# Windowed attention with sinks, then a two-layer MLP, on one core: masks added on PE in batch 0, dummy PE passes, and double-buffered transposed q and k

## The chip, the core and the metric

The kernel runs on one core of a Trainium2 chip. The metric is device microseconds (us) per execution, the median of several runs. The engines are PE (TensorE), DVE (VectorE), ACT (ScalarE), POOL (GpSimd) and SP (SyncE, which here only issues DMAs).

## What is computed

Batch 4, 8 heads, 768 positions, head dimension 64. Each query sees the first 4 positions (the sinks) and the last 128 positions up to its own. The attention output, laid out as 3,072 tokens by 512, goes through an MLP with 2,048 hidden units and a squared ReLU.

```python
scores = q @ k.T / sqrt(64)
keep = is_sink | ((pos_q - pos_k >= 0) & (pos_q - pos_k < 128))
a = softmax(where(keep, scores, -1e9))
x = (a @ v).transpose(0, 2, 1, 3).reshape(3072, 512)
out = relu(x @ w_in) ** 2 @ w_out
```

## The kernel before

The work goes batch by batch (b = 0 to 3). `attention(b)` makes the 512-wide input of batch b's MLP, `layer1` and `layer2` are the MLP. Attention of batch b + 1 is laid between the MLP matmuls of batch b, so that PE has work while ACT and DVE do the softmax.

**Order.** The program is not written in the order in which it runs. Each step is registered with a key (its due time), the engines that may do it with a cost for each, the steps it comes after, and the buffers (`Slot`) that it takes and gives back. `Plan.run` (line 52) then walks a model of the engines, and records at each point the step that can start first. So costs and keys set the order of each engine's instructions; on the chip each engine runs its own instructions in that order, and waits on semaphores for the others.

**Inputs.** In batches 0 and 1, q and k are loaded in FP32 on SP's queue (`load_qk`, L303), cast to BF16 with the pairs of heads regrouped (`regroup`, tile `qs`, on ACT, DVE or POOL, L186, L188, L190), transposed on PE (`transpose`, tile `pt`, L405) and copied to `qkT_sb` (`unload`). Batch 0 does it in two groups: positions 0 to 511 first (its loads are the first DMAs), then positions 512 to 767, whose loads stand behind the first half of `w_in`. That half is issued on POOL's queue once v's second block of batch 0 has landed (`load_w_in`, L271). In batches 2 and 3 (`NATURAL`) the DMAs do this: POOL's queue loads q, k and v as BF16 (`load_natural`, L335, L342; q and k to tiles `qn`), and SP's queue transposes each 128 positions into `qkT_sb` (`turn`, L379), twelve transfers a batch. There is one `qkT_sb`; the turns of batch b wait until all scores and sink scores of batch b - 1 have been computed (`prev_scores`, `prev_sinks`).

**Attention.** For each 256 positions s and each pair m0 of head pairs: `scores` (tile `ps`, L484) on PE, into two PSUM slots of the pool `att`; `expo` (tile `expm`, L500) on ACT; `domask`, a multiplication with a 0/1 mask on DVE (L509), or two affine_selects on POOL (L202); `values` on PE (tile `po`, L535), with the sinks' part from `es`; `norm` on DVE (L547, L549): two reciprocals and two multiplications into `xn_sb`. The sink scores of a batch are four matmuls (`sink_scores`, tile `pk`, L454); they read all positions of the transposed q. `bridge` (tile `px`, L571) and its copy, or a DMA transpose in batches 2 and 3 (`turn_x`, L560), give `xT`.

**MLP.** `layer1` (tile `pm`, L594), ReLU (L603, L605), square (L610); `layer2` (tile `py`, L630), copy to `osb`, store (L647). PSUM has two pools, `att` and `den`, of two slots each.

```python
prev_scores = [ops[x] for x in ops if x[0] == "scores" and x[1] == b - 1]
...
ops["turn", b, ti, t] = op(
    at(0.1 * s), {"sp": 1.25}, turn, dma=0.3, reads=[qn_slot[b, ti, s]],
    after=[ops["qk", b, ti, t]] + prev_scores + prev_sinks)
...
load_w_in(0, 5.7, ("v", 0, 1))
load_w_in(1, 8.7)
```

Of the kernel before, what the change touches and what calls it, by code (L numbers as in the profile page):

```python
# [18 lines left out]
DMA_LATENCY = 2.0  # L19


class Slot:


    def __init__(self, pool, readers):
        self.pool, self.readers, self.end = pool, readers, 0.0
# [10 lines left out]
class Plan:  # L37
# [14 lines left out]
    def run(self):  # L52
# [71 lines left out]
def kernel(  # L124
# [11 lines left out]
    nc = tc.nc  # L136
# [16 lines left out]
    sizes = dict(att=2, den=2, qr=5, qs=6, vf=3, qn=8, expm=8, r=3, osb=2)  # L153
# [10 lines left out]
    mask0 = consts.tile([128, 2, 4, 128], BF16)  # L164
    head_rows = consts.tile([32, H, 1], BF16)
# [6 lines left out]
    qkT_sb = consts.tile([128, NP, 2, S], BF16)  # L172
# [27 lines left out]
    def triangles(e_tile, i, n):  # L200

        nc.gpsimd.affine_select(  # L202
            out=e_tile, in_=e_tile, compare_op=ALU.is_ge, fill=0.0, base=i - 1,
            pattern=[[0, n], [1 if i else -1, 128]], channel_multiplier=-1 if i else 1,
        )

    def fill(e):
        nc.vector.memset(ident, 1.0)
        nc.vector.memset(tri, 1.0)
# [11 lines left out]
    def build_triangles(e):  # L221
        for i in range(2):
            triangles(tri[:, i:i + 1, :], i, 1)

# [18 lines left out]
    c_tri = op(-0.9, {"pool": 0.6}, build_triangles)  # L243
    c_masks = op(-0.9, {"dve": 1.5}, build_masks, after=[c_tri])
    c_sinks = op(-0.8, {"pool": 0.5}, build_head_rows)
# [78 lines left out]
    def load_natural(b, s, older_values):  # L324

        begun = [ops["layer1", b - 2, 0, 0], w_out_op[3]]
        for ti in (1, 0):
            sl = qn_slot[b, ti, s] = Slot("qn", 2)
            for i in range(2):
                t = 2 * s + i  # L330

                def run(e, i=i, t=t, ti=ti):
                    if i == 0:
                        qn_t[b, ti, s] = work["qn"].tile([128, 2, DM], BF16, name="qn", tag="qn")
                    return [nc.gpsimd.dma_start(  # L335
                        out=qn_t[b, ti, s][:, i, :].rearrange("p (h d) -> p h d", d=D),
                        in_=(q, k)[ti][b, :, 128 * t:128 * t + 128, :].rearrange("h p d -> p h d"))]
                o = dma_op("pool", ("qk", b, ti, t), run, 64 * 0.032, takes=[sl] if i == 0 else ())
# [10 lines left out]
    def attention(b, key):  # L349
# [5 lines left out]
        prev_scores = [ops[x] for x in ops if x[0] == "scores" and x[1] == b - 1]  # L355
        prev_sinks = [ops[x] for x in ops if x[0] == "sinks" and x[1] == b - 1]
# [402 lines left out]
```

## Time and profile before

| what | value |
|---|---|
| median of 3 runs | 247.62 us (247.38 to 248.05) |
| the profiled execution | 247.71 us, of which the span of the trace is 246.0 us |
| PE busy | 217.8 us (89%) |
| ACT, DVE, POOL busy | 119.7 us (49%), 110.5 us (45%), 48.2 us (20%) |
| PE's idle time by stretch: 0 to 24, 24 to 54, 54 to 104, 104 to 117, 117 to 200, 200 to 246 us | 10.9, 3.5, 0.5, 7.0, 1.1, 5.2 us |
| mean granted TensorE clock | 0.979 |
| DMA | 29.68 MB, mean 121 GB/s |

PE is the engine with the most work, so the reading starts at the stretches in which it is idle or slow: at the start, where data arrive, and between 104 and 117 us. Some matmul records are missing in the last stretch, so its idle time is overstated. The granted clock is recorded from about 25 us on; ahead of that the durations of equal matmuls tell which of the two levels (1.2 and 2.4 GHz) was in force.

### The profile page before, as it was taken

What the parts mean: (1) busy time and instruction counts of PE and PEld (TensorE: products, weight loads), DVE (VectorE), ACT (ScalarE), POOL (GpSimd) and SP (SyncE); (2) the same over time, 40 slices, a digit from 0 to 9 for tenths busy, and PEclk for the clock granted to TensorE, in tenths of its full rate; (3) what the DMA queues carried; (4) which work ended last, traced back from release to release, by engine and by line L of the source; (5) the groups of instructions that cost most, each with busy time, mean ns of one, the idle gap of its engine ahead of it and who ended that gap; (6) DMA issues with size and microseconds to landing.
All of it is one profiled execution on the core that took longest, in us unless ns stands there. A gap on an engine that the chain in (4) does not pass through costs nothing.

```text
span 246.0 us, 4463 instructions
## 1 busy us (share of the span) xinstructions
PE 217.8 (89%) x1838; PEld 130.5 (53%) x1860; DVE 110.5 (45%) x251; ACT 119.7 (49%) x137; POOL 48.2 (20%) x67
## 2 busy tenths in 40 slices
PE   1469789979999999944999999999999999999983
PEld 1246668967454654422854554467555544584431
DVE  6476379776434527540343352573633413431010
ACT  3477367887335464740433534765731335560110
POOL 2021153492632933552000000000000100000000
PEclk9999979999999999995999999999999999999999
DMA  5979999899991999999801266644004222000051
GB/s 172 284 130 212 270 323 319 181 173 184 149 131 7 217 110 170 149 154 149 41 18 26 89 171 87 171 85 45 0 3 128 88 43 85 1 3 0 0 209 47
DMA packets 82500, 29.68 MB, mean 121 GB/s; under 512 B 70192, under 2 KB 78384, under 8 KB 82480
## 3 DMA queue, kind: packets, MB, share of 16 engines
q0 software_dynamic: 40608, 8.92, 51.3%
q1 hardware_dynamic: 41872, 20.49, 35.6%
q8 instruction: 14, 0.23, 0.4%
q14 instruction: 6, 0.05, 0.1%
HBM read 27.30 MB, written 6.29 MB: 137 GB/s over the span
## 4 chain that ended last, share of the span: by engine, by line
PE 77%; DMA 14%; ACT 3%; issue 2%; DVE 1%; SPq 1%; DVEq 0%; ACTq 0%
PE py L630 33%; PE pm L594 32%; PE po L535 5%; PE ps L484 4%; DMA w_in_sb<-in_moe_w_in_dram 4%; DMA qr<-in_k_dram 4%; DMA qkT_sb<-qn 4%; DMA vf<-in_v_dram 3%; ACT r L603 2%; PE pk L454 2%; PE pt L405 1%; ACT qs L186 1%; DVE qkT_sb L188 1%; SPq L379 1%; PE px L571 1%
## 5 line engine op out<-in xcount | busy, mean ns | idle before, releaser
L594 PE MATMUL pm<-xT,w_in_sb 128*128 128x256 bf16 (+1 forms) x570 | 89.7, 313 | 1.0 <-ACT r L603 0.7
L630 PE MATMUL py<-w_out_sb,gT_sb 128*128 128x512 bf16 x369 | 86.3, 379 | 1.9 <-DVE osb L188 0.8
L594 PEld LDWEIGHTS <-w_in_sb 128*128 128x128 bf16 x576 | 56.6, 100 | 30.3 <-issue 3.4
L603 ACT ACTIVATE r<-pm 128x1024 bf16<-128x1024 f32 x45 | 46.0, 1026 | 40.9 <-PE pm L594 35.1
L630 PEld LDWEIGHTS <-gT_sb 128*128 128x128 bf16 x384 | 35.6, 98 | 41.2 <-issue 3.0
L500 ACT ACTIVATE expm<-ps 128x1024 bf16<-128x1024 f32 (+1 forms) x48 | 43.1, 950 | 27.4 <-PE ps L484 27.4
L610 DVE TENSOR_TENSOR gT_sb<-r 128x1024 bf16<-128x1024 bf16 x48 | 33.7, 703 | 48.7 <-ACT r L603 48.6
L509 DVE TENSOR_TENSOR expm<-expm,mask 128x1024 bf16<-128x1024 bf16 (+1 forms) x44 | 28.1, 641 | 24.9 <-ACT expm L500 23.8
L202 POOL TENSOR_SCALAR_AFFINE_SELECT expm<-expm 128x512 bf16<-128x512 bf16 x8 | 5.3, 690 | 97.4 <-ACT expm L500 97.4
L186 ACT ACTIVATE osb<-py 128x1024 f32<-128x1024 f32 (+1 forms) x10 | 9.6, 959 | 23.8 <-PE py L630 16.3
L535 PEld LDWEIGHTS <-expm 128*128 128x128 bf16 x352 | 18.4, 101 | 4.6 <-DVE xn_sb L549 0.3
L484 PE MATMUL ps<-qkT_sb 64*128 64x128 bf16 (+1 forms) x256 | 16.0, 258 | 3.9 <-DVE qkT_sb L188 2.3
L535 PE MATMUL po<-v,expm 128*128 128x65 bf16 x352 | 19.3, 200 | 0.0
L549 DVE TENSOR_TENSOR xn_sb<-po,rc 128x256 bf16<-128x256 f32 x48 | 18.1, 418 | 0.0
L405 PE MATMUL pt<-ident,qs 128*128 128x128 bf16 x96 | 9.1, 250 | 8.7 <-ACT qs L186 5.2
L484 PEld LDWEIGHTS <-qkT_sb 64*128 64x128 bf16 x256 | 9.1, 99 | 13.0 <-issue 10.2
L188 DVE COPY osb<-py 128x1024 f32<-128x1024 f32 (+2 forms) x4 | 3.6, 892 | 26.0 <-PE py L630 26.0
L535 PE MATMUL po<-vs,es 128*128 128x65 bf16 x128 | 14.0, 195 | 0.0
L335 POOL DMA_DIRECT2D qn<-in_k_dram x12 | 10.6, 892 | 13.6 <-DMA qkT_sb<-qn 8.3
L547 DVE RECIPROCAL rc<-po 128x4 f32<-128x4 f32 x48 | 5.9, 165 | 15.3 <-PE po L535 15.3
L405 PEld LDWEIGHTS <-qs 128*128 128x128 bf16 x96 | 6.8, 111 | 10.5 <-ACT qs L186 5.5
L535 PEld LDWEIGHTS <-es 128*128 128x128 bf16 x128 | 12.3, 101 | 0.0
(40 smaller groups left out, 98.6 us busy)
## 6 DMA issues: line engine op xcount, KB each, us to landing
out_dram<-osb SPq DMA_DIRECT2D x11, 512.0 KB, 3.2
vf<-in_v_dram SPq DMA_DIRECT2D x12, 256.0 KB, 7.9
w_in_sb<-in_moe_w_in_dram POOLq DMA_DIRECT2D x2, 1024.0 KB, 11.1
w_out_sb<-in_moe_w_out_dram POOLq DMA_DIRECT2D x4, 512.0 KB, 8.9
qr<-in_k_dram SPq DMA_DIRECT2D x2, 768.0 KB, 9.0
qr<-in_q_dram SPq DMA_DIRECT2D x2, 768.0 KB, 10.6
qn<-in_k_dram POOLq DMA_DIRECT2D x12, 128.0 KB, 11.0
qn<-in_q_dram POOLq DMA_DIRECT2D x12, 128.0 KB, 10.9
```

The source lines that it names most:

```text
L186: nc.scalar.activation(out=dst, in_=src, func=AF.Copy)
L335: return [nc.gpsimd.dma_start(out=qn_t[b, ti, s][:, i, :].rearrange("p (h d) -> p h d", d=D), in_=(q, k)[ti][b, :, 128 * t:128 * t + 128, ...
L405: nc.tensor.matmul(pt[:, ti, 128 * t:128 * t + 128], lhsT=qs[:, t, :, :], rhs=ident, is_transpose=True, start=(t == 0), stop=(t == n - 1))
L484: nc.tensor.matmul(ps[:, h2, o:o + w], lhsT=qkT_sb[r, m, 1, 128 * c:128 * c + 128], rhs=qkT_sb[r, m, 0, 128 * qb:128 * qb + w], start=(i = ...
L500: nc.scalar.activation(out=x[:, :, o:512], in_=bank_t["s", b, s, m][:, :, o:512], func=AF.Exp, scale=scale)
L509: nc.vector.tensor_mul(x[:, :, o:512], x[:, :, o:512], mk[:, :, o:512])
L535: nc.tensor.matmul(pv[:, i, h2, :], lhsT=lhsT, rhs=rhs, start=(n_ == 0), stop=(n_ == len(mms) - 1))
L549: nc.vector.tensor_tensor(out=xn_sb[:, 2 * s + i, 128 * m0:128 * m0 + 256].rearrange("p (j h d) -> p j h d", j=2, d=D), in0=pv[:, i, :, :, ...
L594: nc.tensor.matmul(pm[:, i, :], lhsT=w_in_sb[:, kb, 128 * fb:128 * fb + 128], rhs=xT[:, kb, c0:c0 + cw], start=(kb == 0), stop=(kb == NKB ...
L603: nc.scalar.activation(out=r, in_=bank_t.pop(tag), func=AF.Relu)
L610: (nc.vector if e == "dve" else nc.gpsimd).tensor_mul(gT_sb[:, fbs[0]:fbs[0] + n, c0:c0 + cw], r, r)
L630: nc.tensor.matmul(pm[:, i, :], lhsT=gT_sb[:, fb, 128 * t:128 * t + 128], rhs=w_out_sb[:, fb, :], start=(fb == 0), stop=(fb == NFB - 1))
```

## The change

Six things are changed.

1. Batch 0, first group ("biased"): the mask is no longer multiplied in after exp. PE first writes it as a bias (0 or -30,000) into the PSUM bank, as a matmul of `ident` with a table `bias` or `bias0`, and the scores are accumulated on top. Two such matmuls (of 512 columns, or 384 for the first 256 positions) for each head pair, 16 in all; the eight mask multiplications of these positions go. POOL builds the tables.
2. Scores of batch 0 are planned one head pair at a time, and in the first group they, and the other PSUM tiles of that group, may take a slot of either pool.
3. `warm` puts dummy matmuls (128 by 128, `ident` with `ident`) in front of a step that the plan starts before 34 us, as many as fill half of the gap that the plan sees on PE there, at most 40. Into BF16 tiles (`pt`, `px`) they are transposes. The program has 80 of them: 40 ahead of the first transposes, then 8, and the others in groups of 1 to 13.
4. `qkT_sb` becomes two tiles, `qkT_all`, one for even and one for odd batches; the turns of batch b come after the scores of batch b - 2. The tiles `qn` now hold all six blocks and come from the pool `qr`.
5. `norm` is one reciprocal and one multiplication.
6. The first half of `w_in` stands behind v's first block of batch 0 and no longer behind its second. Keys and costs of masks, casts and norms are altered.

```diff
+WARM_UNTIL = 34.0
...
+                    if len(s.pools) > 1:
+                        s.pool = min(s.pools, key=lambda p: min(free[p], default=1e9))
...
+            self.now, self.gap = start, start - engine.get(e, 0.0)
             o.run(e)
...
-    qkT_sb = consts.tile([128, NP, 2, S], BF16)
+    qkT_all = [consts.tile([128, NP, 2, S], BF16, name=f"qkT{i}") for i in range(2)]
...
+    def warm(dst):
+        if P.now < WARM_UNTIL:
+            for _ in range(min(40, int(0.5 * P.gap / 0.056))):
+                nc.tensor.matmul(dst, lhsT=ident, rhs=ident, start=True, stop=True,
+                                 is_transpose=dst.dtype == BF16)
...
+    def build_bias(e):
+        for i in range(2):
+            triangles(bias.rearrange("p (j i) c -> p i j c", i=2)[:, i], i, 2, -30000.0)
+        nc.gpsimd.tensor_copy(out=bias0, in_=bias)
+        nc.gpsimd.memset(bias0[0:NSINK, 1:3, :], 0.0)
...
-            sl = qn_slot[b, ti, s] = Slot("qn", 2)
+            if s == 0:
+                qn_slot[b, ti] = Slot("qr", NT)
...
-        prev_scores = [ops[x] for x in ops if x[0] == "scores" and x[1] == b - 1]
-        prev_sinks = [ops[x] for x in ops if x[0] == "sinks" and x[1] == b - 1]
+        prev_scores = [ops[x] for x in ops if x[0] == "scores" and x[1] == b - 2]
+        prev_sinks = [ops[x] for x in ops if x[0] == "sinks" and x[1] == b - 2]
...
+        qkT_sb = qkT_all[b % 2]
...
+            biased = b == 0 and g == 0
...
-                    banks = [Slot("att", 1) for _ in range(2)]
+                    banks = [Slot(("att", "den") if b == 0 and g == 0 else "att", 1) for _ in range(2)]
...
+                            if biased:
+                                o = segs[0][0]
+                                for h2 in range(2):
+                                    nc.tensor.matmul(
+                                        ps[:, h2, o:512], lhsT=ident,
+                                        rhs=(bias if s else bias0).rearrange("p j c -> p (j c)")[:, o:512],
+                                        start=True, stop=False)
...
+                        if biased:
+                            masked.append(ex)
+                            continue
-                        masked.append(op(at(fm + 0.03), {"pool": 1.5, "dve": 0.8} if s else {"dve": 0.6},
+                        masked.append(op(at(fm + 0.03), {"pool": 1.35, "dve": 0.75} if s else {"dve": 0.58, "pool": 1.1},
...
-                        for i in range(2):
-                            nc.vector.reciprocal(out=rc[:, i], in_=pv[:, i, :, :, D:D + 1])
...
+                        nc.vector.reciprocal(out=rc, in_=pv[:, :, :, :, D:D + 1])
...
-    load_w_in(0, 5.7, ("v", 0, 1))
+    load_w_in(0, 5.7, ("v", 0, 0))
...
-            at(0, 0.0, 1.0, "den")
+            at(0, 0.0, 1.0, ("den", "att"))
```

**How the change moves instructions, first place: the start of batch 0.** PE before, at its first scores (`pt` are transposes, `ps` scores):

```order
L405 MATMUL pt<-ident,qs 128x128
L484 LDWEIGHTS qkT_sb
L484 MATMUL ps<-qkT_sb 128x256
L484 LDWEIGHTS qkT_sb
L484 MATMUL ps<-qkT_sb 128x256
L484 LDWEIGHTS qkT_sb
L484 MATMUL ps<-qkT_sb 128x128
```

PE now, at the same place (L197 is `warm`, L515 the bias):

```order
L432 MATMUL pt<-ident,qs 128x128
L197 LDWEIGHTS ident
L197 MATMUL ps<-ident 128x128
L515 LDWEIGHTS ident
L515 MATMUL ps<-bias_92,ident 128x384
L515 LDWEIGHTS ident
L515 MATMUL ps<-bias_92,ident 128x384
```

Behind these come the scores as before. In the first group all scores and the sink scores now stand ahead of all values on PE, and all values and both bridges ahead of the first `pm`; before, the first 32 `pm` came after the first bridge and half of the second block's values.

POOL before, from its first constant to the first loads of `w_in`:

```order
L218 AFFINE_SELECT ident<-ident 128x128
L202 AFFINE_SELECT tri<-tri 128x128 x2
L234 AFFINE_SELECT head_rows<-head_rows 32x8
L237 AFFINE_SELECT head_rows<-head_rows 32x8
L271 DMA w_in_sb<-in_moe_w_in_dram 128x4x1024 x2
```

POOL now:

```order
L235 AFFINE_SELECT ident<-ident 128x128
L218 AFFINE_SELECT bias<-bias 128x2x128 x2
L245 COPY bias_92<-bias 128x512
L246 MEMSET bias_92 4x256
L257 AFFINE_SELECT head_rows<-head_rows 32x8
L260 AFFINE_SELECT head_rows<-head_rows 32x8
L218 AFFINE_SELECT tri<-tri 128x128 x2
L206 CAST qs<-qr 128x512
L295 DMA w_in_sb<-in_moe_w_in_dram 128x4x1024 x2
```

The tables and one cast of q now stand ahead of the `w_in` loads on POOL.

**Second place: the turns of batch 2.** SP before, from v's last loads of batch 1 to the last turn of batch 2 (`qkT_sb<-qn`):

```order
L320 DMA vf<-in_v_dram 128x8x64 x6
L647 DMA out_dram<-osb 128x2x512 x2
L379 DMA_TRANSPOSE qkT_sb<-qn 128x4x128 x4
L647 DMA out_dram<-osb 128x2x512
L379 DMA_TRANSPOSE qkT_sb<-qn 128x4x128 x8
```

SP now, from the same loads (`qkT_103` is the tile of batches 0 and 2, `qkT_104` that of 1 and 3):

```order
L344 DMA vf<-in_v_dram 128x8x64 x6
L405 DMA_TRANSPOSE qkT_103<-qn 128x4x128 x4
L694 DMA out_dram<-osb 128x2x512
L405 DMA_TRANSPOSE qkT_103<-qn 128x4x128
L694 DMA out_dram<-osb 128x2x512
L405 DMA_TRANSPOSE qkT_103<-qn 128x4x128 x5
L694 DMA out_dram<-osb 128x2x512
L405 DMA_TRANSPOSE qkT_103<-qn 128x4x128 x2
```

Ten of the twelve turns now stand ahead of the third store of batch 0, where four did.

PE before, around the sink scores of batch 2:

```order
L594 MATMUL pm<-xT_109,w_in_sb 128x256
L454 LDWEIGHTS kblk_97
L454 MATMUL pk<-qkT_sb,kblk_97 128x512
L454 LDWEIGHTS kblk_97
L454 MATMUL pk<-qkT_sb,kblk_97 128x512
```

PE now:

```order
L641 MATMUL pm<-xT_109,w_in_sb 128x512
L482 LDWEIGHTS kblk_96
L482 MATMUL pk<-qkT_103,kblk_96 128x512
L482 LDWEIGHTS kblk_96
L482 MATMUL pk<-qkT_103,kblk_96 128x512
```

The sink scores stood behind 16 of the 128x256 `pm` and all 64 of the 128x512 `pm` of batch 1, with 16 `ps` of batch 2 ahead of them; now they stand behind 56 of the 128x512 `pm`, with 8 `ps`.

## Rows read from the trace of the kernel before

**Rows 1.** Stretches: from:to, us, PE, PEld, DVE, ACT, POOL busy, PEclk, DMA, GB/s

```profile
12.00:15.00 3.00, 2.20 (x20) 1.76 (x19) 1.95 (x4) 1.62 (x4) 1.42 (x2) 1.00 0.69 146
54.00:104.00 50.00, 49.53 (x434) 27.86 (x439) 25.31 (x57) 27.34 (x31) 24.02 (x29) 1.00 1.93 141
104.00:117.00 13.00, 6.03 (x33) 3.47 (x32) 3.19 (x5) 4.18 (x6) 5.24 (x6) 0.74 2.24 151
117.00:200.00 83.00, 81.91 (x713) 46.48 (x724) 37.08 (x87) 38.74 (x41) 1.22 (x2) 1.00 0.36 73
```

**Rows 2.** Chain of waits, start: start us, us, what

```profile
5.14 8.14 DMA vf<-in_v_dram
...
13.58 8.88 DMA w_in_sb<-in_moe_w_in_dram
...
22.51 6.04 DMA qr<-in_k_dram
...
45.09 0.74 PE po L535 x24
...
73.81 0.45 PE px L571 x8
```

**Rows 3.** Timeline of PE, start: start us, us, instructions, idle before and releaser

```profile
11.81 1.89 PE L405 MATMUL pt<-ident,qs 128*128 128x128 bf16 x16
...
16.67 1.04 PE L454 MATMUL pk<-qkT_sb,kblk 128*128 128x256 bf16 x4 [0.35 <-DVE kblk L438]
...
29.04 0.28 PE L405 MATMUL pt<-ident,qs 128*128 128x128 bf16 x2 [0.98 <-ACT qs L186]
...
31.65 0.94 PE L484 MATMUL ps<-qkT_sb 64*128 64x128 bf16 x12 [0.50 <-DVE qkT_sb L188]
32.52 3.22 PE L594 MATMUL pm<-xT,w_in_sb 128*128 128x256 bf16 x16
```

**Rows 4.** Timeline of PE, the longest wait

```profile
114.17 1.86 PE L454 MATMUL pk<-qkT_sb,kblk 128*128 128x512 bf16 x4 [6.97 <-DMA qkT_sb<-qn]
```

**Rows 5.** Chain of waits, middle

```profile
103.18 0.46 PE ps L484 x8
...
105.19 8.72 DMA qkT_sb<-qn
...
114.17 1.86 PE pk L454 x4
116.03 4.10 PE pm L594 x32
...
120.50 1.75 PE pm L594 x16
...
166.71 0.86 PE pk L454 x4
167.58 3.49 PE pm L594 x32
```

**Rows 6.** Timeline of SP's queue, turns and stores

```profile
80.80 9.49 SPq L379 DMA_TRANSPOSE qkT_sb<-qn  x4
92.29 0.38 SPq L647 DMA_DIRECT2D out_dram<-osb  x1
92.77 14.76 SPq L379 DMA_TRANSPOSE qkT_sb<-qn  x8
```

**Rows 7.** Line L379, all turns

```profile
DMA to landing us min/median/max: 2.4/4.2/11.7
```

**Rows 8.** Line L320, v's first two blocks of batch 0

```profile
L320 SPq DMA_DIRECT2D vf<-in_v_dram x2: 508/1685/2862, 4.6 to 5.1; - x2
...
DMA to landing us min/median/max: 7.6/7.9/8.1
```

**Rows 9.** Timeline of DVE, first cast of batch 0's second group

```profile
29.48 0.29 DVE L188 CAST qs<-qr 128x256 bf16<-128x256 f32 x1 [3.81 <-DMA qr<-in_q_dram]
```

**Rows 10.** Page, costliest groups: exp

```profile
L500 ACT ACTIVATE expm<-ps 128x1024 bf16<-128x1024 f32 (+1 forms) x48 | 43.1, 950 | 27.4 <-PE ps L484 27.4
```

More of the change, by code (lines that the diff above doesn't have):

```diff
@@ L164 @@
     mask0 = consts.tile([128, 2, 4, 128], BF16)
+    bias = consts.tile([128, 4, 128], BF16)
+    bias0 = consts.tile([128, 4, 128], BF16)
     head_rows = consts.tile([32, H, 1], BF16)
@@ L197, in after_dma, with triangles @@
         )
-    def triangles(e_tile, i, n):
+    def triangles(e_tile, i, n, fill=0.0):
         nc.gpsimd.affine_select(
-            out=e_tile, in_=e_tile, compare_op=ALU.is_ge, fill=0.0, base=i - 1,
+            out=e_tile, in_=e_tile, compare_op=ALU.is_ge, fill=fill, base=i - 1,
             pattern=[[0, n], [1 if i else -1, 128]], channel_multiplier=-1 if i else 1,
@@ L208, in fill @@
         nc.vector.memset(ident, 1.0)
+        nc.vector.memset(bias, 0.0)
         nc.vector.memset(tri, 1.0)
@@ L327, in load_natural, with run @@
         for ti in (1, 0):
[L328 removed]
+            if s == 0:
+                qn_slot[b, ti] = Slot("qr", NT)
             for i in range(2):
                 t = 2 * s + i
[L332 to L334 removed]
+                def run(e, t=t, ti=ti):
+                    if t == 0:
+                        qn_t[b, ti] = work["qr"].tile([128, NT, DM], BF16, name="qn", tag="qr")
                     return [nc.gpsimd.dma_start(
[L336 removed]
+                        out=qn_t[b, ti][:, t, :].rearrange("p (h d) -> p h d", d=D),
                         in_=(q, k)[ti][b, :, 128 * t:128 * t + 128, :].rearrange("h p d -> p h d"))]
[L338 removed]
+                o = dma_op("pool", ("qk", b, ti, t), run, 64 * 0.032, takes=[qn_slot[b, ti]] if t == 0 else ())
                 o.after += begun
@@ L401, in transpose @@
                     pt = bank_t[b, m, g] = bank(bs, "pt", [128, 2, 1024], BF16)
+                    warm(pt[:, 0, 0:128])
                     for ti in (1, 0):
@@ L452, in sink_scores @@
                 ps = bank_t["sink", b] = bank(bk, "pk", [128, 512], FP32)
+                warm(ps[:, 0:128])
                 for m in range(NP):
@@ L487, in scores @@
                                         rhs=qkT_sb[r, m, 0, 128 * qb:128 * qb + w],
-                                        start=(i == 0), stop=(i == len(segs) - 1))
-                    sc = op(at(fm), {"pe": 0.65}, scores, takes=banks,
+                                        start=(i == 0 and not biased), stop=(i == len(segs) - 1))
+                    sc = []
+                    for ms in ((m0,), (m0 + 1,)) if b == 0 else ((m0, m0 + 1),):
+                        sc.append(op(
+                            at(fm), {"pe": len(ms) * (0.7 if biased else 0.28) + 0.1}, lambda e, f=scores, ms=ms: f(e, ms),
+                            takes=[banks[m - m0] for m in ms],
                             after=[ops["turn", b, ti, t] for ti in (0, 1)
                                    for t in range(max(0, 2 * s - 1), 2 * s + 2)] if b in NATURAL else
-                            [ops["copy", b, m, ti, gg] for m in (m0, m0 + 1) for ti in (0, 1)
-                             for gg in range(g + 1)])
-                    ops["scores", b, s, m0] = sc
+                            [ops["copy", b, m, ti, gg] for m in ms for ti in (0, 1) for gg in range(g + 1)]))
+                        ops["scores", b, s, ms[0]] = sc[-1]
                     masked = []
@@ L520, in values @@
                         po = bank_t["o", b, s, m0] = bank(bo, "po", [128, 2, 512], FP32)
+                        warm(po[:, 0, 0:128])
                         for j, m in enumerate((m0, m0 + 1)):
@@ L568, in bridge @@
                     px = bank_t["x", b] = bank(bx, "px", [128, NKB, 256], BF16)
+                    warm(px[:, 0, 0:128])
                     for i in range(2):
```

48 lines of the change are left out of this document (27 added, 21 removed).

## The prediction

> **What bounds the kernel now.** I read the stretches first, then the chain of waits, then the timelines where the chain leaves PE. Between 54 and 104 us, and again from 117 to 200, PE is busy 49.5 of 50 and 81.9 of 83 us [rows 1]: in these stretches a change that costs PE nothing changes nothing. What can be won lies in two other places.
>
> *The start.* The chain runs through transfers: v's second block lands at 13.28, only then the first half of `w_in` is issued (13.58) and lands at 22.46, and only then the loads of batch 0's second group go out, the first of which lands at 28.55 [rows 2]. Its q lands at about 29.45, where DVE's cast ends its wait [rows 9]. PE waits there 0.98 us, with small gaps behind [rows 3]. So up to about 30 us this gate of transfers decides, as long as PE has done its part ahead of it. PE also runs at its lower level there: four sink scores of 256 columns take 1.04 us at 16.67, more than batch 3's four of 512 columns (0.86), and 16 `pm` of 256 columns take 3.22 us at 32.52 against 1.75 at 120.50 [rows 3, 5], which is the 1.2 against the 2.4 GHz level.
>
> *104 to 117 us.* PE stands still for 6.97 us ahead of batch 2's sink scores, until the last turn of its q and k has landed [rows 4]. That turn was issued at 105.19 and took 8.72 us [rows 5]. Behind the wait the granted clock is down, 0.74 on the mean [rows 1]: the sink scores take 1.86 us and the next 32 `pm` 4.10, where batch 3's take 0.86 and 3.49 [rows 5].
>
> **The change, part by part.** The sum is made against the profiled execution, 247.71 us, which is 0.09 above the median.
>
> *Two transposed tiles.* The turns no longer wait for batch 1's scores. If PE finds batch 2's tile complete, the wait (6.97) goes, and so does the lower level behind it (1.86 - 0.86 + 4.10 - 3.49 = 1.61): **8.6 us**. Is it complete? PE comes to these sink scores earlier, since 16 `pm` of 256 columns, 8 of 512 (as many columns, so 1.75 us each) and 8 `ps` (0.46) have moved behind them: 1.75 + 1.75 + 0.46 = 3.96 [rows 5]. PE was done with what stood ahead at 114.17 - 6.97 = 107.20, so it would come at 103.2, less what the start gains. On SP's queue ten turns now stand ahead of batch 0's third store, and the last two behind it. That store goes at 92.29 [rows 6], and it hangs on PE's progress, so it too moves by the start's gain. The five turns between the second and third store fit: with the transfers crowded, four took 9.49 us [rows 6] and there are 12 us. The last turn is then issued at about 92.29 + 0.48 + 1.4 = 94.2 and, with the 8.72 us of the crowded case [rows 5], lands at 102.9, 0.3 us ahead of PE. The ends are 2.4 and 11.7 us to landing [rows 7]: nothing waits, or 2.7 us are left. I take no wait, because the nearest row is the one in the same crowd; the crowd stays, since the loads of batch 3, whose tiles now come from `qr`, no longer wait for the turns and go out earlier.
>
> *The gate at the start.* `w_in` now waits for v's first block, issued at 4.6, which lands after 7.6 us, at 12.2 and not 13.28 [rows 8]. POOL's new table work and the cast ahead of it end before that: the cast's q has been transposed on PE from 11.81 on [rows 3]. Between 12 and 15 us the transfers ran at 146 GB/s, the lowest of the start [rows 1], so there is room. All that hangs on `w_in` comes up to 1.1 us earlier; I take 1.0 (ends 0, if the other v blocks only share the same rate, and 1.1).
>
> *PE ahead of the gate.* Now all values and both bridges of the first group stand ahead of the first `pm`. That is 24 `po` (0.74) and 8 `px` (0.45) [rows 2] which were done behind the gate: **1.2 us** off the path, if PE gets through in time. The 0.50 us wait for a copy ahead of the next scores [rows 3] goes too, as 16 `pm` now stand in that place. PE must start its 32 `pm` (3.5 us) by 28.4 - 3.5 = 24.9. From 11.81 on it has 16 transposes, five scores with their bias, the sink scores, 72 `po`, 16 `px` and 31 of the 80 dummies. At the lower level: transposes 1.9; bias, priced by the 512-column sink scores (1.86 / 4 = 0.465 each), 6 x 0.465 + 4 x 0.35 = 4.2; scores 5 x 0.47 = 2.4 [rows 3]; sink scores 1.0; `po` twice 2.2; `px` 1.8; dummies 31 x 0.118 = 3.7. Together 19.4, so the start of `pm` would be 31.2. At the upper level the same list is 9.3 us by the rows at that level (0.215 for a 512-column pass, 0.056 for a dummy [rows 5, 2]), so 21.1, plus a microsecond or two for exp, whose eight passes of 0.95 [rows 10] now come one after the other without masks between. I take a clock that rises about half way, 25, near the gate: the bias passes are dense matmuls, and the stretch from 11.81 on has no wait for data. The 49 dummies ahead of 11.81 cost nothing: the scores of the first pair wait for q in any case.
>
> The rows do not show whether transposes raise the clock; after 16 of them back to back at 118 ns the sink scores at 16.67 still ran at the lower level [rows 3]. The Trainium skill ("TensorE: Matmul & The Clock Gate", Part 4: PE-mode transpose) says that a transpose does not count as PE activity in the way a matmul does, and the full rate does not engage for it; 61 of the 80 dummies are transposes, and by that rule they warm nothing. By the rule the 31.2 is nearer than the 25; the result of that is the first rival below.
>
> *Given back.* The start's gain so far is 1.0 + 1.2 + 0.5 = 2.7. Batch 1's casts, transposes and copies follow at about 45 us, and they are bound by their loads, which are only 1.0 earlier, and by copies on ACT and DVE. Between those bounds (1.0 and 2.7) I take **2.0**. Its outer ends: 1.4 lost, if `pm` starts at 31.2 (35.2 for the same work that before is done at 30.36 + 1.2 + 0.5 + 1.8 = 33.9, where 1.8 is the cost of the lower level at 31 to 35 us: 3.22 - 1.75 + 0.94 - 0.55, about); and 4.5, if PE never falls to the lower level either.
>
> *Nothing for the rest.* The eight masks leave DVE, which is busy 21 to 25 us in 50, and the exps on ACT stay. The merged norm spares two of four DVE instructions, beside a PE that is full [rows 1], so 0; without that cover it would be worth at most 2 x 0.29 us a norm (DVE's cast of as many elements [rows 9]).
>
> Sum: 247.7 - 8.6 - 2.0 = 237.1; against the median 237.0.
>
> **The rivals.**
>
> *1. PE stays at the lower level at the start* (16%). The dummies and bias passes are 19.4 us of PE work that end behind the gate. For it: the transposes above. Against it: the ten bias passes of this stretch are ordinary matmuls of 384 and 512 columns, the longest work that PE has had by then. The 1.4 us are lost in place of the 2.0 won: 247.7 - 8.6 + 1.4 = 240.5.
>
> *2. The last turns land late, by a little* (13%). For it: the margin of 0.3 us is smaller than anything I can read. With 11.7 us to landing [rows 7] PE waits 2.7 us: 239.7; with a microsecond or two of further delay on SP's queue 241.
>
> *3. The last turns land later than before, relative to PE: slower* (3%). SP's queue, ahead of batch 2's sink scores. The tiles `qn` no longer hold the loads of batch 3 back, so these fill the DMA engines first. As PE comes 3.96 us of work earlier, the break-even is a landing at 114.17 - 3.96 = 110.2; beyond it every microsecond is lost, and the start's gain is swallowed by the wait. If the last turn goes out at 105.19 as before and takes 11.7, it lands at 116.9: 247.7 + 2.7 + 4.0 = 254.4. Against it: ten turns are already through by then.
>
> *4. PE keeps the upper level from the first group on* (6%): the start gains 4.5, and the time is 234.5.
>
> **How the numbers follow.** The forecast case has 62%, 235 to 239 alone. With rival 4 below and rivals 1 and 2 above, 8 in 10 lie between 234.2 and 241.2. A measurement of this kernel can tell about 0.3% (0.7 us) from no change. Slower by more than that: rival 3, and a little for an unseen wait, 3%; within it 2%; faster 95%.
>
> **What would show it.** Right: no wait of PE at batch 2's sink scores, which then take 0.86 us, and a granted clock of 1.0 from 104 to 117 us; `w_in` issued at 12.2 to 12.5; the first `pm` at 23 to 26; the casts of the second group at 28.4. Wrong: PE still waits for `qkT<-qn` more than 3 us; or the first `pm` comes at 30; or a new wait of some microseconds between 54 and 104 us or from 117 to 200, where there is none now.

## The result and the profile after

The changed kernel takes **239.64 us** (median of 4 runs, 237.86 to 241.01), the kernel before 247.84 us beside it; the ratio is 0.9661, interval 0.958 to 0.9742. Timed again later, it took 238.90 us (6 runs, 236.89 to 242.25) against 247.99: 0.9593, interval 0.9552 to 0.9633. Medians here are of all runs, and ratios leave out runs more than 1.5% above the fastest of their kernel. The forecast was 237.0 in a range of 234.2 to 241.2. The kernel is faster, as forecast: by 8.2 and 9.1 us in the medians and by 8.4 and 10.1 in the ratios, where 10.6 were forecast. The profiled execution is at the upper side of these runs: 240.65 us, span 238.9 (before 246.0), so 7.1 us of span are to be accounted for.

The stretches of the changed kernel, with the columns of [rows 1] (the first is new, it holds the gate of transfers):

```profile
24.00:54.00 30.00, 24.29 (x268) 19.69 (x266) 18.43 (x33) 18.14 (x23) 12.13 (x17) 0.89 0.96 240
54.00:104.00 50.00, 48.99 (x425) 27.62 (x430) 25.80 (x45) 27.38 (x31) 26.00 (x31) 1.00 1.85 159
104.00:117.00 13.00, 12.26 (x114) 9.07 (x116) 7.40 (x15) 7.54 (x9) 4.37 (x5) 1.00 2.01 138
117.00:200.00 83.00, 81.69 (x672) 43.99 (x681) 32.90 (x56) 39.94 (x43) 0.00 (x0) 1.00 0.40 73
```

From 104 to 117 us PE is now busy for 12.26 us and not for 6.03, and the granted clock is 1.00 and not 0.74. But in the stretch from 24 to 54 the clock is 0.89. The kernel before had there:

```profile
24.00:54.00 30.00, 26.50 (x319) 22.23 (x317) 21.15 (x43) 21.11 (x28) 14.38 (x20) 0.94 1.07 255
```

So by these two clocks an estimate of 6.6 us of the 30 were at the lower level (0.11 of 30, twice), where it was 3.6 us before.

PE's timeline of the changed kernel, at the start and at batch 2's sink scores, answers to [rows 3] and [rows 4]:

```profile
1.49 4.02 PE L197 MATMUL pt<-ident 128*128 128x128 bf16 x40 [1.49 <-POOL ident L235]
5.35 0.39 PE L432 MATMUL pt<-ident,qs 128*128 128x128 bf16 x4
...
11.16 1.07 PE L432 MATMUL pt<-ident,qs 128*128 128x128 bf16 x16
...
16.89 0.60 PE L482 MATMUL pk<-qkT,kblk 128*128 128x256 bf16 x4
...
22.21 3.67 PE L641 MATMUL pm<-xT,w_in_sb 128*128 128x256 bf16 x32
28.45 0.28 PE L432 MATMUL pt<-ident,qs 128*128 128x128 bf16 x2 [2.57 <-DVE qs L204]
29.35 0.82 PE L432 MATMUL pt<-ident,qs 128*128 128x128 bf16 x6 [0.62 <-DVE qs L204]
30.45 3.57 PE L641 MATMUL pm<-xT,w_in_sb 128*128 128x256 bf16 x16 [0.27 <-ACT r L650]
...
104.69 1.04 PE L482 MATMUL pk<-qkT,kblk 128*128 128x512 bf16 x4 [1.22 <-DMA qkT<-qn]
```

Three things are to be seen. The sixteen transposes at 11 us take 1.07 us where they took 1.89 [rows 3], and the first sink scores 0.60 where they took 1.04: PE is at its upper level early. It is through with everything ahead of the gate early: the first 32 `pm` start at 22.21. Then it has nothing to do for 2.57 us, and behind that the next sixteen `pm` take 3.57 us, as at the lower level [rows 3 and 5: 3.22 there and 1.75 at the upper]. At the sink scores of batch 2 the wait is 1.22 us, where it was 6.97 [rows 4].

The chain of waits of the changed kernel, pieces at the gate, at batch 1's first layer-one products and at batch 2's sink scores, answers to [rows 2] and [rows 5]:

```profile
12.22 9.94 DMA w_in_sb<-in_moe_w_in_dram
...
22.70 6.28 DMA qr<-in_q_dram
...
53.52 3.49 PE pm L641 x32
...
96.49 8.15 DMA qkT<-qn
...
104.69 1.04 PE pk L482 x4
```

The same step of batch 1 in the kernel before:

```profile
53.24 3.49 PE pm L594 x32
```

SP's queue in the changed kernel, from its second store on, answers to [rows 6]:

```profile
82.18 1.10 SPq L694 DMA_DIRECT2D out_dram<-osb  x1
83.39 10.60 SPq L405 DMA_TRANSPOSE qkT<-qn  x5
94.08 0.56 SPq L694 DMA_DIRECT2D out_dram<-osb  x1
94.73 7.49 SPq L405 DMA_TRANSPOSE qkT<-qn  x4
```

And the cast that ends DVE's wait for the second group's q, which answers to [rows 9]:

```profile
29.00 0.29 DVE L204 CAST qs<-qr 128x256 bf16<-128x256 f32 x1 [0.61 <-DMA qr<-in_q_dram]
```

**Four pieces.** Four points cut the span: this cast, batch 1's first `pm`, batch 2's sink scores, the end. The cast comes 0.48 us earlier (29.00 for 29.48). From there to batch 1's first `pm` it takes 24.52 us and not 23.76: 0.76 lost. From there to the sink scores 51.17 and not 60.93: 9.76 gained. From there to the end 134.21 and not 131.83: 2.38 lost, since work was moved behind them. The sum is 7.10. The whole gain lies at the sink scores, and the start gave nothing: 53.52 for 53.24.

### The profile page after: what moved, and what is told of

Read it like the earlier page. It is cut to its first block, busy times and chain, and to the rows that moved or that the text cites. A ratio compares the mean times of both kernels' runs of the same rounds, so it can differ in the third digit from the quotient of the medians.

```text
span 238.9 us, 4585 instructions
## 1 busy us (share of the span) xinstructions
PE 221.3 (93%) x1932; PEld 133.9 (56%) x1956; DVE 106.1 (44%) x201; ACT 117.5 (49%) x133; POOL 48.2 (20%) x68
## 4 chain that ended last, share of the span: by engine, by line
PE 76%; DMA 14%; ACT 3%; DVE 2%; SPq 1%; issue 1%; ACTq 0%; DVEq 0%
PE py L677 33%; PE pm L641 31%; PE po L583 5%; DMA w_in_sb<-in_moe_w_in_dram 4%; PE ps L522 4%; DMA qkT<-qn 3%; DMA vf<-in_v_dram 3%; DMA qr<-in_q_dram 3%; PE pt L432 2%; PE pk L482 1%; DMA qr<-in_k_dram 1%; SPq L405 1%; ACT r L650 1%; ACT expm L541 1%; DVE qkT L204 1%
## 5 line engine op out<-in xcount | busy, mean ns | idle before, releaser
L650 ACT ACTIVATE r<-pm 128x1024 bf16<-128x1024 f32 x48 | 49.2, 1026 | 41.9 <-PE pm L641 35.8
L550 DVE TENSOR_TENSOR expm<-expm,mask 128x1024 bf16<-128x1024 bf16 (+1 forms) x38 | 24.7, 649 | 31.3 <-ACT expm L541 30.4
L202 ACT ACTIVATE osb<-py 128x1024 f32<-128x1024 f32 (+1 forms) x11 | 10.6, 964 | 32.9 <-PE py L677 25.4
L583 PEld LDWEIGHTS <-expm 128*128 128x128 bf16 x352 | 17.0, 97 | 4.3 <-DVE xn_sb L595 0.6
L583 PE MATMUL po<-v,expm 128*128 128x65 bf16 x352 | 17.9, 194 | 0.4 <-DVE xn_sb L595 0.4
L595 DVE TENSOR_TENSOR xn_sb<-po,rc 128x512 bf16<-128x512 f32 x24 | 16.6, 691 | 0.8
L522 PE MATMUL ps<-qkT 64*128 64x128 bf16 (+1 forms) x256 | 14.8, 238 | 0.5 <-ACT qkT L202 0.4
L522 PEld LDWEIGHTS <-qkT 64*128 64x128 bf16 x256 | 8.1, 94 | 10.9 <-issue 10.2
L360 POOL DMA_DIRECT2D qn<-in_k_dram x12 | 10.6, 890 | 11.1 <-DMA v<-in_v_dram 6.6
L204 DVE COPY osb<-py 128x1024 f32<-128x1024 f32 (+2 forms) x3 | 2.3, 780 | 22.9 <-PE py L677 22.9
L367 POOL DMA_DIRECT2D v<-in_v_dram x12 | 10.7, 898 | 7.4 <-PE pm L641 3.3
L206 POOL CAST qs<-qr 128x256 bf16<-128x256 f32 (+2 forms) x9 | 6.3, 703 | 28.4 <-DMA qr<-in_k_dram 19.9
L594 DVE RECIPROCAL rc<-po 128x8 f32<-128x8 f32 x24 | 4.9, 204 | 15.6 <-PE po L583 15.4
## 6 DMA issues: line engine op xcount, KB each, us to landing
qn<-in_q_dram POOLq DMA_DIRECT2D x12, 128.0 KB, 11.9
```

The source lines that it names most:

```text
L202: nc.scalar.activation(out=dst, in_=src, func=AF.Copy)
L367: return [nc.gpsimd.dma_start(out=v_sb[b % 2][:, :, t, 0:D], in_=v[b, :, 128 * t:128 * t + 128, :].rearrange("h p d -> p h d"))]
L522: nc.tensor.matmul(ps[:, h2, o:o + w], lhsT=qkT_sb[r, m, 1, 128 * c:128 * c + 128], rhs=qkT_sb[r, m, 0, 128 * qb:128 * qb + w], start=(i = ...
L550: nc.vector.tensor_mul(x[:, :, o:512], x[:, :, o:512], mk[:, :, o:512])
L583: nc.tensor.matmul(pv[:, i, h2, :], lhsT=lhsT, rhs=rhs, start=(n_ == 0), stop=(n_ == len(mms) - 1))
L595: nc.vector.tensor_tensor(out=xn_sb[:, 2 * s:2 * s + 2, 128 * m0:128 * m0 + 256].rearrange("p i (j h d) -> p j i h d", j=2, d=D), in0=pv[: ...
```

## The experiments

**Theory:** the second transposed tile makes the gain, less a remaining wait for late turns; what the other parts win ahead of the gate ends in idle time there, because the transfers decide when the start ends. **Rivals:** the rest of the change wins a part of the time too; or the start would win, and the lower clock behind the idle time takes it back. Each run has its own expectation, in which "theory A" and "theory B" are those of that run.

### Two tiles alone, and all but the second tile

The kernel before with two tiles, and with `qn` in the pool `qr` for all blocks:

```diff
-    qkT_sb = consts.tile([128, NP, 2, S], BF16)
+    qkT_all = [consts.tile([128, NP, 2, S], BF16, name=f"qkT{i}") for i in range(2)]
...
-        prev_scores = [ops[x] for x in ops if x[0] == "scores" and x[1] == b - 1]
+        prev_scores = [ops[x] for x in ops if x[0] == "scores" and x[1] == b - 2]
```

(and likewise for `prev_sinks`.)

> The kernel before with the two transposed tiles alone (and the tiles qn from the pool qr). Theory A: they carry nearly the whole gain, since the wait of 6.97 us at batch 2's sink scores and the lower clock behind it go (up to 8.6 us, with 1 to 2 us of wait left as in the changed kernel): 240 us, between 239 and 241.5. Rival B: the start of batch 0 (bias, dummies, gate) carries several microseconds of the gain: this kernel stays above 243.

Measured: 240.17 us (239.74 to 240.62), ratio 0.9686, interval 0.9635 to 0.9736. The row of its sink scores of batch 2, on PE's timeline:

```profile
104.57 1.04 PE L456 MATMUL pk<-qkT,kblk 128*128 128x512 bf16 x4 [1.32 <-DMA qkT<-qn]
```

The changed kernel with one tile and the old order behind it:

```diff
-    qkT_all = [consts.tile([128, NP, 2, S], BF16, name=f"qkT{i}") for i in range(2)]
+    qkT_all = [consts.tile([128, NP, 2, S], BF16, name="qkT0")] * 2
...
-        prev_scores = [ops[x] for x in ops if x[0] == "scores" and x[1] == b - 2]
+        prev_scores = [ops[x] for x in ops if x[0] == "scores" and x[1] == b - 1]
```

(and likewise for `prev_sinks`.)

> The changed kernel with one transposed tile again, everything else kept. Theory A: the wait of about 7 us at batch 2's sink scores is back, and the time is 246 to 248.5. Rival B: the rest of the change is worth several microseconds by itself: below 244.

Measured: 247.37 us (245.16 to 248.61), ratio 0.997, interval 0.9927 to 1.0012. The same row:

```profile
113.18 1.86 PE L482 MATMUL pk<-qkT,kblk 128*128 128x512 bf16 x4 [6.34 <-DMA qkT<-qn]
```

The two interventions agree that the second tile makes most of the gain. The new pool of `qn` is in both kernels, so it does not make it by itself. The tiles alone (0.9686) are not told apart from the first measurement of the whole change (0.9661); the later one (0.9552 to 0.9633) ends just below their interval (0.9635 to 0.9736). They were not timed side by side, so it stays open whether the rest of the change adds up to some 2 us on top of the tiles. Without the second tile it brings nothing that a measurement tells. With one tile the long wait and the lower level behind it (1.86 us) are back. That nothing is a balance, though: in its profile (a span of 246.3 us) the sink scores come 0.99 us earlier than before (113.18 for 114.17), and the first 32 `pm` behind them take 1.35 us longer than the 4.10 before [rows 5], with a granted clock of 0.86 from 117 to 124 us where it was 0.99:

```profile
115.04 5.45 PE pm L641 x32
```

### No dummies

```diff
-        if P.now < WARM_UNTIL:
+        if P.now < 0.0:
```

> The changed kernel without its 80 dummy passes. If dummies that are transposes do not raise the clock, nothing moves: the first layer-1 matmul at 22.2 us as in the changed kernel. If they do raise it (theory A, from the recorded level of 1.0 from 4.92 us on), PE runs at the lower level until its bias passes fill it, and the first layer-1 matmul comes at 24 to 28 us. Even so the time should be within 1.5 us of the changed kernel (238 to 241), because the gate of transfers at 28 us hides up to 2.6 us of it. Rival: the dummies are on the path and carry gain: above 241.5.

Measured: 241.0 us (238.19 to 241.36), ratio 0.9696, interval 0.9628 to 0.9764: not told apart from the changed kernel. PE's timeline:

```profile
11.33 1.07 PE L432 MATMUL pt<-ident,qs 128*128 128x128 bf16 x16
...
21.95 3.65 PE L641 MATMUL pm<-xT,w_in_sb 128*128 128x256 bf16 x32
27.59 0.28 PE L432 MATMUL pt<-ident,qs 128*128 128x128 bf16 x2 [1.99 <-DVE qs L204]
```

Without dummies PE is at the upper level at 11 us as well (passes that add the mask stand ahead). The first `pm` start at 21.95, not at 24 to 28 as expected if the dummies raise the clock, and PE waits at the gate as in the changed kernel. No effect of the dummies on the time is shown.

### Work for PE at the gate

If the lower clock behind PE's idle time takes the gain back, dummies that fill that time should return it. 44 and 10 transposes of `ident` into the bank of the second group's first pair:

```diff
                     for ti in (1, 0):
+                        for _ in range({1: 44, 0: 10}[ti] if b == 0 and g == 1 and m == 0 else 0):
+                            nc.tensor.matmul(pt[:, ti, 0:128], lhsT=ident, rhs=ident, start=True, stop=True,
+                                             is_transpose=True)
```

> The changed kernel with 54 more dummy transposes in PE's idle time ahead of the transposes of batch 0's second group (44 before the k part, 10 before the q part of the first head pair). Theory A: PE's idle time there is what brings the clock down from 28.8 to 35.6 us, and this costs about 3 us; with the idle time filled the clock stays at its upper level, and the time is 236 to 238. Rival: the fall has another cause, or what is won is lost again at batch 1's copies: 239 to 240 as the changed kernel.

The runs disagreed: 237.38 us in the profiled one, at a granted clock of 1.0, and 241.16, 241.33 and 241.63 in the others; no ratio could be given. So it was timed again with more runs.

> The kernel with 54 more dummies at the gate once more, since its profiled execution took 237.4 us at a clock of 1.0 and its three timed ones 241.2 to 241.6. If filling the idle time is worth what the profile shows: 237 to 238.5, below the changed kernel by 1.5 to 3 us. If not: 239.5 to 241.5, as the changed kernel or above.

Measured: 238.52 us (237.26 to 240.53), ratio 0.9623, interval 0.9584 to 0.9663, which overlaps both intervals of the changed kernel. The profile of this second one shows what was wanted, no wait ahead of the second group's transposes and a clock of 1.00 in the whole stretch:

```profile
27.81 0.28 PE L435 MATMUL pt<-ident,qs 128*128 128x128 bf16 x2
27.92 0.72 PE L431 MATMUL pt<-ident 128*128 128x128 bf16 x10
```

Its stretch, where before the last three columns were 0.94, 1.07 and 255:

```profile
24.00:54.00 30.00, 26.93 (x350) 23.50 (x350) 21.99 (x38) 19.83 (x25) 14.86 (x19) 1.00 1.07 250
```

In the profiles the remedy works; in the times it is not told apart from the changed kernel.

### The last turns

A second theory on the remaining wait: POOL, which also issues the loads of `qn`, has masks of batch 1 in its way. They go to DVE.

```diff
-                        masked.append(op(at(fm + 0.03), {"pool": 1.35, "dve": 0.75} if s else {"dve": 0.58, "pool": 1.1},
+                        masked.append(op(at(fm + 0.03), ({"dve": 0.75} if b == 1 else {"pool": 1.35, "dve": 0.75}) if s else {"dve": 0.58, "pool": 1.1},
```

> The changed kernel with batch 1's masks on DVE alone, so that no affine_select stands among POOL's loads of q, k and v for batches 2 and 3 (in the changed kernel POOL waits 7.2 us there, and the transfers idle). Theory A: the wait of 1.2 us that is left at batch 2's sink scores comes from turns that share the transfers with these late loads; earlier loads leave less to share, the last turn lands 3 us or more earlier, the wait is gone, and the time falls by 1 to 1.5 us against the changed kernel (238 to 239). Rival: the last two turns are held by the third store ahead of them on SP's queue, and land as late as before: the same time, and PE still waits 1 us or more.

Measured: 239.79 us (237.23 to 243.36), ratio 0.9636, interval 0.9569 to 0.9703. The wait is no shorter:

```profile
103.11 1.04 PE L482 MATMUL pk<-qkT,kblk 128*128 128x512 bf16 x4 [1.56 <-DMA qkT<-qn]
```

In the changed kernel loads of `qn` stand on POOL behind a mask that waits 7.22 us for its exp; here they do not, and the wait on PE is still there. So the masks on POOL are not needed for it. Its SP queue shows the pattern of the changed kernel: five turns in 10.44 us, the third store at 92.41, 0.09 us behind their end, and then the last turns.

```profile
81.88 10.44 SPq L405 DMA_TRANSPOSE qkT<-qn  x5
92.41 0.53 SPq L694 DMA_DIRECT2D out_dram<-osb  x1
```

Both together, the dummies at the gate and no masks of batch 1 on POOL:

> Both: the dummies at the gate and batch 1's masks off POOL. If the two gains are real and add up: 235.5 to 237.5, and the best so far. If the wait at batch 2's sink scores only grows by what PE gains ahead of it (the turns land at their own time), the second alone gives little and the two together more than the sum: still 236 to 237.5. If neither holds: 239 to 241.

Measured: 240.15 us (238.18 to 242.98), ratio 0.967, interval 0.9624 to 0.9717. This is the case in which neither holds: no gain of either is seen in the time.

### Masks multiplied, as before

The passes that add the mask are taken back, two tiles and dummies stay:

```diff
-            biased = b == 0 and g == 0
+            biased = False
```

> The changed kernel with batch 0's masks multiplied in after exp again (no bias passes on PE), dummies kept. Theory A: the first layer-1 matmul moves by less than 2.5 us from 22.2, PE waits for the gate of transfers all the same, and the time is that of the changed kernel within 1 us (239 to 241). Rival: the bias passes carry gain, because the masks delay the values on DVE: above 241.5.

Measured: 236.85 us (236.26 to 239.92), ratio 0.9546, interval 0.951 to 0.9582. That is below both times that were expected, and it looked like 2 to 3 us won by a PE that comes to the gate later: the first `pm` start at 23.79, and there is no wait at the gate:

```profile
27.29 0.28 PE L432 MATMUL pt<-ident,qs 128*128 128x128 bf16 x2
28.20 0.51 PE L432 MATMUL pt<-ident,qs 128*128 128x128 bf16 x6 [0.62 <-DVE qs L204]
```

It was therefore timed again beside the changed kernel, and without dummies (the edits of both sections above).

> The changed kernel as it is, for a comparison on one chip with the next two. Both theories: 238 to 241 us; in its trace a wait of over 1.5 us on PE between the sixteen transposes of the second group's first pair's banks (about 28 to 29 us from the start) and a stretch of some 7 us at half the clock behind it.

> The changed kernel with the first two rounds of tokens masked by multiplication as before, dummies kept. Theory A (the passes that add the mask let PE reach the end of its work too early, it stands idle for the transfer of w_in and q, and the clock falls behind that): 236.3 to 237.5 us, 2 to 3 us under the changed kernel in the same rounds, first layer-one products at 23.5 to 24 us, no half clock before batch 1. Theory B (the earlier 236.85 was a lucky set of runs, the kernels are alike): within 1 us of the changed kernel.

> The previous kernel without the dummy passes: two tiles, scores by single pairs, merged norm, masks multiplied. Theory A: if only the order of the start matters, dummies bring nothing here either: 236.3 to 238 us, clock up by 10 us from the start. Theory B (dummies are needed so that products run at full rate when the masks are multiplied): first products 1 us or more later than with dummies and a time of 238.5 us or more.

Measured: the changed kernel 238.90 us (0.9593, 0.9552 to 0.9633; in its profile a wait of 2.19 us at the gate and a clock of 0.94 for the stretch, so by estimate 3.6 us at the lower level where some 7 were expected), masks multiplied 238.25 (236.6 to 241.61; 0.9578, 0.9542 to 0.9614), masks multiplied without dummies 239.78 (237.62 to 240.33; 0.9646, 0.9603 to 0.9688). The earlier 236.85 did not come back: masks multiplied and masks added lie within 1 us of each other, as theory B of that run had it. Nor was its profile as expected, for the clock fell at the gate, 0.94 for the stretch, after a wait of only 0.86 us:

```profile
28.24 0.28 PE L432 MATMUL pt<-ident,qs 128*128 128x128 bf16 x2 [0.86 <-DVE qs L204]
```

The median without dummies is above the 238.5 us that theory B of that run named, and its first `pm` start at 24.25, 0.53 us later than with them (23.72). But the intervals of the two overlap, and its profile at the gate shows a clock of 1.00; that the dummies help there is not shown.

One more run, to part the clock from the transfers: masks multiplied, with the dummies at the gate.

> The changed kernel with the first rounds' masks multiplied (no passes that add a mask) and with 44 and 10 dummy transposes more in the bank of the second group's first pair. Theory A (what spreads the times of the two-tile kernels over 4 us is whether the clock falls behind PE's idle time at that place): PE has neither idle time nor a reason for a lower clock there; mean granted clock 0.997 or more in nearly every run, median 236.3 to 237.3 us, highest under 239 us. Theory B (the spread comes from when the loads of w_in, q and k land, whatever PE does): median 238 to 240 us, spread 4 us, also at a clock of 1.0.

Measured: 240.56 us (238.61 to 241.38), ratio 0.9693, interval 0.965 to 0.9735. This is nearer to theory B: in three runs with a granted clock of 0.999 or 1.0 the time was 239.9 to 241.4 us, though the median is 0.6 us above the range it named and the six runs lie within 2.8 us of each other, not 4. The profiled one has no wait at the gate and no lower clock, and yet a span of 238.2 us. Its chain of waits:

```profile
23.40 6.21 DMA qr<-in_q_dram
```

The second group's q landed at 29.61, against 27.82 in the best profile of masks multiplied (a span of 235.4):

```profile
21.54 6.28 DMA qr<-in_q_dram
```

### What all profiles say together

The four points of the result, of the kernel before and of every profile with two tiles, from the same rows as there (DVE's cast of the second group's q, batch 1's first `pm` in the chain, batch 2's sink scores with the wait ahead of them, the end of the span; the clock is that of the stretch from 24 to 54 us):

| kernel | cast | to `pm` | clock | to sink scores, less the wait | wait | to the end | span |
|---|---|---|---|---|---|---|---|
| before | 29.48 | 23.76 | 0.94 | 53.96 | 6.97 | 131.83 | 246.0 |
| changed | 29.00 | 24.52 | 0.89 | 49.95 | 1.22 | 134.21 | 238.9 |
| changed, again | 28.83 | 23.29 | 0.94 | 49.95 | 1.07 | 134.26 | 237.4 |
| two tiles alone | 29.57 | 23.74 | 0.94 | 49.94 | 1.32 | 134.03 | 238.6 |
| no dummies | 28.14 | 24.79 | 0.89 | 50.46 | 1.86 | 134.25 | 239.5 |
| gate filled | 27.61 | 22.22 | 1.00 | 49.94 | 1.67 | 134.26 | 235.7 |
| gate filled, again | 27.97 | 22.34 | 1.00 | 49.94 | 0.94 | 134.21 | 235.4 |
| no POOL masks | 28.82 | 22.79 | 1.00 | 49.94 | 1.56 | 134.29 | 237.4 |
| both | 29.49 | 22.33 | 1.00 | 49.94 | 0.49 | 134.25 | 236.5 |
| masks multiplied | 27.84 | 22.20 | 1.00 | 49.94 | 1.14 | 134.28 | 235.4 |
| masks multiplied, again | 28.79 | 23.69 | 0.94 | 49.94 | 1.59 | 134.19 | 238.2 |
| the same, no dummies | 29.87 | 22.68 | 1.00 | 49.94 | 1.20 | 134.21 | 237.9 |
| the same, gate filled | 29.64 | 22.30 | 1.00 | 49.94 | 1.59 | 134.73 | 238.2 |

The span of a two-tile kernel is the sum of a landing (27.6 to 29.9), a piece that goes with the clock (22.2 to 22.8 at 1.00, 23.3 to 23.7 at 0.94, 24.5 to 24.8 at 0.89), a wait (0.5 to 1.9), and two pieces that hardly vary, 49.94 and about 134.2, with one exception each. The 50.46 has its reason in a second fall: without dummies the clock was 0.84 from 52 to 58 us, and the 32 `pm` at 52.93 took 4.01 us for 3.49. The 134.73 has none that was found. The changed kernel itself differed from run to run: the spans were 235.2 and 235.3 us at a granted clock of 1.0 and 238.9 and 239.3 at 0.982, but also 237.0 at 0.984, so the clock is not the whole of it. The landing varies as well, and no variant set out to move it: with `w_in` issued where the change puts it, between 11.8 and 12.9 us, it landed between 20.1 and 22.9, where the two kernels with the old issue have 22.46 and 21.92. With one or two profiles of each kernel a variant's effect on it can't be told from chance. No reason in the code is shown for differences of a microsecond or so between the medians, and none of the variants is shown to beat the changed kernel.

## Why the prediction was right, and where it was not

**The two tiles: right, but for the wait.** The step was 6.97 + 1.61 = 8.6. The profile gives 9.76 - 2.38 = 7.38 us, which is 8.6 less the wait of 1.22 that is left. Its parts hold: the work moved behind the sink scores, taken as 3.96, is 53.96 - 49.95 = 4.01, and what the end of the kernel gets back, taken as 1.61 for the lower level, is 4.01 - 2.38 = 1.63.

**The step that failed there** is "the last turn is then issued at about 92.29 + 0.48 + 1.4 = 94.2 and ... lands at 102.9, 0.3 us ahead of PE". PE came at 103.47; the row of the last turn is 96.49 + 8.15 = 104.64. The landing took about what was taken (8.15 for 8.72), the issue was 2.3 us late. I let the third store hang on PE. Its copy had ended at 92.55:

```profile
91.53 1.02 ACT L202 ACTIVATE osb<-py 128x1024 f32<-128x1024 f32 x1
```

But the store goes at 94.08, 0.09 us behind the end of five turns which took 10.60 us and had started at 83.39: on this queue the store stood behind the turns, and the last turns behind the store. I had asked whether the five fit into the 12 us between two stores and answered yes, though by the four in 9.49 us they take 11.9; and I did not ask when the first of them could begin. It stood behind the second store (82.18), and so the fifth ended at 93.99, past the 92.29 that I had for the third store.

The held store is not the whole cause. In the kernel with two tiles alone the store goes at 92.36, as I had it and as soon as its copy has ended, and PE still waits 1.32 us:

```profile
91.31 1.02 ACT L186 ACTIVATE osb<-py 128x1024 f32<-128x1024 f32 x1
```

```profile
92.36 0.37 SPq L649
...
92.82 2.21 SPq L381
...
95.13 9.39 DMA qkT<-qn
```

There the turn ahead of the last took 2.21 us where I had 1.4, and the last one 9.39 where I had 8.72, so it landed at 104.52. In both kernels the last turn landed some 1.6 to 1.7 us later than the 102.9 of the sum; what sets the pace of the turns in the crowd is open, since no variant set out to alter the order on SP. This is rival 2 in kind, at less than half its price. It was kept at 13% for a margin that was "smaller than anything I can read"; with such a margin a part of the wait belonged in the sum.

**The gate of transfers: half.** Taken 1.0, measured 0.48. `w_in` went out as forecast, at 12.22. The step that failed is "so there is room": the transfer took 9.94 us where it had taken 8.88, and landed at 22.16 for 22.46. The 146 GB/s of [rows 1] had told of little traffic in a stretch, not of room for one transfer more. The 0.48 is one draw: over the eleven profiles of the table with this issue the cast came at 28.7 us on the mean (27.61 to 29.87), 0.8 us ahead of the two with the old issue (29.48 and 29.57). So 1.0 is near what many executions have on the mean, and this one had half of it.

**PE ahead of the gate: a third of the term at most.** 1.2 + 0.5 were taken for work that PE has done earlier. At the same clock of the stretch, 0.94, the piece from the cast to batch 1's `pm` is 23.76 before and 23.74 with two tiles alone, against 23.29 in the changed kernel and 23.18 (52.89 - 29.71) with one tile: 0.5 to 0.6 us. In the changed kernel its chain is on PE from 30.45 us on, but near its end it changes between PE's transposes of batch 1 and copies on ACT and DVE, and while a copy runs PE is off the chain:

```profile
46.74 0.68 PE pt L432 x12
...
47.45 0.82 ACT qkT L202
...
48.29 0.97 DVE qkT L204
...
49.30 0.84 PE pt L432 x12
```

In the kernel with two tiles alone the end of this piece runs through v's blocks of batch 1 and ACT, with PE off the chain altogether until 51.61 us:

```profile
42.60 4.59 DMA vf<-in_v_dram
...
48.84 0.96 ACT v L186
```

So the bound that I named under "given back", loads and copies, is there in the chains. Which of them took how much of the 1.7 us is not shown.

**The clock at the start: wrong in my favour, and of no use.** I took the first `pm` at 25, with 21.1 and 31.2 as ends; it came at 22.21. Rival 1 (its 35.2 less 33.9 is 1.3, not 1.4) fell: PE was at the upper level by 5.35 us. But between 22.21 and the gate the only work is 32 `pm`, so coming 2.8 us earlier turned into idle time, 2.57 us for 0.98 before [rows 3]. In the profiled execution some 6.6 us at the lower level followed, 3.6 before, which by my estimate costs up to 1.5 us more (half of the difference). **The step that failed in the sum** is "Between those bounds (1.0 and 2.7) I take 2.0": the profile has 53.24 - 53.52, 0.28 lost, and the sum had no term for a clock that falls again behind PE's wait at the gate. With a clock of 1.00 it would have been, by an estimate from the table, the landing's 0.48 and about 1.0 to 1.5, near the forecast. So rival 4, in which PE keeps the upper level, came true in some runs, though not its 234.5: two of the changed kernel at a granted clock of 1.0 took 236.9 and 237.1 us. In the profiled execution the start's 2.0 are missing and a wait of 1.22 us is left; that its time still lies within the range is owed to the width of the range and not to the sum.

**The rest at nothing: not contradicted.** The masks, the merged norm, the order of the scores, the dummies and the gate together are a ratio of 0.997, interval 0.9927 to 1.0012 (the kernel with one tile): at most 1.8 us, for the start's 2.0 and the rest together. With two tiles they may be worth more, as said there.

**The rule behind rival 1 fell with it.** PE had done nothing but the forty transposes of its timeline above, from 1.49 us on, when four transposes at 5.35 took 0.39 us; before, four took 0.61, as in this row of its timeline:

```profile
4.21 0.61 PE L405 MATMUL pt<-ident,qs 128*128 128x128 bf16 x4 [4.21 <-ACT qs L186]
```

The two kernels with masks multiplied show it without the passes that add the mask: the first sink scores took 0.61 us (at 17.32) with the dummies and 1.04 without. The Trainium skill ("TensorE: Matmul & The Clock Gate", Part 4: PE-mode transpose) states that a transpose does not count as PE activity as a matmul does and that the full rate does not engage for it; the trace disagrees, with 0.39 us for 0.61.

## What to carry to other kernels

Work that is moved ahead of a gate is worth what the gate itself moves, and the rest is idle time: price a start by the landing that ends it, and ask what an engine does between being done and that landing. Where a transfer is asked to land just ahead of its reader, walk its queue from the first instruction on, with the time each takes in the crowd of that place; a margin of a fraction of a microsecond belongs in the sum as a likely wait. Before a variant is believed to win a microsecond, cut the spans at a few common points: here two pieces were alike to 0.3 us in nearly all kernels, and the spread lay in one landing, one fall of the clock and one wait.

## What the runs showed of the hardware that was not expected

**Forty transposes back to back raise TensorE's clock.** In the changed kernel it was at the upper level by 5.35 us, as told. In five of the other profiles with the same forty it came a little later: the next eight transposes, from 5.73 or 5.74 us on, still took 1.07 to 1.21 us, where eight take 0.61 at the upper level. Without the dummies and with passes that add the mask it was there at 11 us (sixteen transposes in 1.07 us). With neither dummies nor such passes, in the kernel with masks multiplied and no dummies, the same sixteen and the sink scores still ran at the lower level:

```profile
11.29 1.89 PE L432 MATMUL pt<-ident,qs 128*128 128x128 bf16 x16
...
17.68 1.04 PE L482 MATMUL pk<-qkT,kblk 128*128 128x256 bf16 x4 [2.04 <-DVE kblk L465]
```

**The fall at the gate does not follow the length of the wait there.** It fell behind waits of 2.57 us and of 0.86 us, and stayed up behind waits of 1.88 (no POOL masks) and 1.49 us (masks multiplied, no dummies). In all four profiles in which dummies filled the gate it stayed up. In the timed runs of those kernels a granted clock of 0.983 to 0.993 came in some too; where it fell in these is not known.

**A transfer that is issued earlier need not land earlier by as much.** `w_in`, issued 1.36 us earlier, landed 0.30 us earlier in the profiled execution; over the profiles with this issue its time ran from 8.3 to 10.6 us and its landing from 20.1 to 22.9, against 8.88 and 8.34 us and 22.46 and 21.92 with the old one.
